# Block-sparse attention and a squared-ReLU MLP: rows gathered in even-odd order, keys copied as 32-bit words

## The chip, the cores and the metric

The kernel runs on one core of one Trainium2 chip. A time is the device time of one execution in microseconds (us). The five engines are named as in the profile: PE (TensorE; PEld are its weight loads), DVE (VectorE), ACT (ScalarE), POOL (GpSimd) and SP (SyncE, which here only issues DMAs). A line number such as L654 is that of the kernel before.

## The reference: what is computed

There are 4 batches of 8 heads, 768 positions and 64 values per head. Positions form 24 blocks of 32. A query block sees its own block and its two neighbours, the first and the last block, and three sampled blocks; the first and the last query block see everything. The sampled blocks are an input, so they are known only at run time.

```python
scores = scale * np.matmul(q, k.transpose(0, 1, 3, 2))
...
scores = np.where(mask, scores, -1000000000.0)
...
attn = attn / (np.sum(attn, axis=-1, keepdims=True) + 1e-09)
return np.matmul(attn, v).astype(np.float32)
```

The heads of a position are joined into 512 values, and an MLP follows on all 3072 positions: `h = x @ w_in` (512 to 2048), `r = max(h, 0)`, `(r * r) @ w_out` (2048 to 512).

## The kernel before, in words

**Two ways to do attention.** Batches 0 and 1 are done densely: all scores are computed (`scores`, L490), their exponentials are taken on ACT (`exps`, L501) and multiplied by a 0/1 mask on DVE (`masks`, L508), and `values` (L530) multiplies by v. Each v row carries a 1 besides its 64 values, so the sum of the weights comes out in the same matmul. `normalize` (L538, L540) divides on DVE and writes a buffer `xq`, of which there are `XQ_BUFS = 3`; `x_transp` (L547) turns the result over on PE, and `x_evac` copies it into `xT`, the MLP's input.

Batches 2 and 3 are done sparsely, in 6 tiles each. A tile has four query blocks of 32; tile 5, which comes first, has two inner blocks, and the first and last block of the sequence, which see all keys, fill it up. For each query block a tile gathers 256 keys into a buffer `KG`: 96 of the window, 32 of block 0, 96 of the three sampled blocks, 32 of the last block. `k_window` copies the window's keys (L637), `k_random` the sampled ones at a place held in a register (L654), `k_global` the two fixed blocks once per batch and then spread over the tile (L659, L661). `q_tile` copies the tile's queries into `QG` (L674). `QG` has a zero half for each of the two heads that lie on the 128 partitions, so that one matmul with all 128 partitions (L700) gives both heads' scores of 32 queries: 64 columns.

The values of v are gathered from a copy of v in DRAM, `vd`, into `VG`: `v_window` and `v_global` by DMAs that SP issues (L680, L684), `v_random` by indirect DMAs that POOL issues (L688), with row numbers in `idx`. `blocks_index` works out `idx` and the registers' places with some two dozen small DVE operations (L586 to L602). `s_scores`, `s_exps`, `s_values`, `s_normalize`, `s_transp` and `s_evac` are the sparse tile's counterparts of the dense steps. `s_patch` zeroes the weights of a block that would be counted twice.

**The order of positions.** The transposed q and k of the sparse batches, `QKB`, hold the even positions of a sequence first and then the odd ones, because a DMA transpose on pairs of rows leaves them so. In the kernel before, every copy out of `QKB` puts them back into natural order. `spread` is the destination's view:

```python
def keys_of(b):
    return QKB[b % 2][:, :, 1, :].rearrange("p a (n m) -> p a n m", n=2)
def spread(x):
    return x.rearrange("p a (m n) -> p a n m", n=2)
```

so an inner run of 16 or 48 keys is read from consecutive places and written to every second one.

**The MLP.** `hidden` (L795) multiplies by `w_in`, `relu` (L804 on ACT, L806 on DVE) and `square` (L815 on ACT, L817 on POOL) follow, `output` (L845) multiplies by `w_out`, `out_copy` and `store` bring it out. This work fills PE while attention waits for ACT and DVE.

**What sets the order.** A planner inside the kernel runs when the kernel is built. Every step is a `Task` with the engines that may do it, an estimated duration on each, its predecessors, the buffers that it takes and gives back, a key and sometimes an earliest time. `run_schedule` always issues the task that can start first on its engine and prefers small keys, and chooses the engine for tasks that have a choice: `k_window` between DVE and ACT, `q_tile` between DVE and POOL, `relu`, `square`, the casts and the evacuations likewise. The result is a fixed order of instructions on each engine. Each engine runs its instructions in that order, and the waits between engines are semaphores. The constants at the top (`TILE_AT` with the earliest time of each sparse tile, `VISITS`, `PACE`, `SEEDS`, which breaks ties, and others) shape that order. [...]

Of the kernel before, what the change touches and what calls it, by code (L numbers as in the profile page):

```python
# [12 lines left out]
F32 = mybir.dt.float32  # L13
# [12 lines left out]
def kernel(  # L26
# [37 lines left out]
    QC_BUFS, XQ_BUFS, YS_BUFS, XS_BUFS = 4, 3, 3, 2  # L64
# [26 lines left out]
    AHEAD = {"PE": 0, "DVE": 0.135, "ACT": 0.107, "POOL": 0.0, "SP": 0.0}  # L91
    LEAD = -2.424
    NB_, SLEAD, KACT = 49.137, 6.758, 0.3
    EARLY = (70.906, -88.936, -92.499, 95.336, 115.53, -46.181, 55.274, 166.555)
    TILE_AT = (102.791, 88.778, 40.785, 126.152, 70.33, 71.88, 157.89, 120.037, 118.424, 174.907, 219.536, 219.598)
    VISITS = (-24.404, 17.697, 7.265, 16.177, 0.947, -92.464, 8.409, 18.969, -10.624, 11.589, -49.341, -6.74, 2.02, 7.146, -74.249, -23.742, -110.985, -12.456)
    HOLD, PATIENCE = 0, 13.793
    PACE0, PACE, SINGLE, MASK_AT = 41.973, 1.372, 1, 17.0
# [5 lines left out]
    class Buf:  # L104
        def __init__(self, pool):
# [5 lines left out]
    TIES = 1.955, 1.912  # L111
    SEEDS = (
            850913, 826317, 823543, 823026, 572023, 972473, 867181, 602326, 495681,
            997735, 889080, 648164, 499408, 642303, 291601, 709162, 308345, 66895,
            457299, 405177, 404720, 744698, 807919, 805802)
# [8 lines left out]
    class Task:  # L124
        def __init__(self, engs, key, fn, deps=(), get=(), put=(), after=0.0, mode=None, dma=0.0, late=None, bias={}, port=False,
                     lead=0.0, yields=False, paced=False, quiet=False, mm=0):
# [5 lines left out]
            self.mm, self.us = mm, 0.0  # L132
# [7 lines left out]
    def run_schedule(free, bufs, dma_free, mode=128):  # L140
# [28 lines left out]
        while waiting or ready:  # L169
# [12 lines left out]
            for t in ready:  # L182
# [25 lines left out]
                for e, us in t.engs.items():  # L208
                    r = max([r0, free[e]] + [seen(d, e) - t.lead for d in t.deps])
                    sw = SWITCH if e == "PE" and t.mode and t.mode != mode else 0.0  # L210
                    if (e == "POOL" and not t.quiet) or (e == "DVE" and t.port):
                        p0, p1 = port["DVE" if e == "POOL" else "POOL"]
                        if p0 <= r < p1:
                            us = max(us, p1 - r + us - HEAD)
# [21 lines left out]
            if (e == "POOL" and not t.quiet) or (e == "DVE" and t.port):  # L236
                port[e] = (at, end)
                o = "DVE" if e == "POOL" else "POOL"
                more = end + last[o].us - HEAD - port[o][1] if last[o] and at <= port[o][0] < end else 0.0
# [81 lines left out]
    QG = [consts.tile([P, HP, 4, 2, block], BF, name=f"QG{i}") for i in range(2)]  # L321
    warm = QG[0].rearrange("p a i h q -> p (a i h q)")[:, 0:256]
# [32 lines left out]
    make_identity(nc, identb)  # L355

# [224 lines left out]
    def blocks_index():  # L581
# [4 lines left out]
        steps = [lambda: V.tensor_copy(out=rb, in_=picked_of),  # L586
                 lambda: TS(out=at16.rearrange("p (q r) -> p q r", r=n_rand), in0=picked_of[0:1], scalar1=block // 2, scalar2=None, op0=AOP.mult),
# [40 lines left out]
    def keys_of(b):  # L628
        return QKB[b % 2][:, :, 1, :].rearrange("p a (n m) -> p a n m", n=2)

    def spread(x):
        return x.rearrange("p a (m n) -> p a n m", n=2)

    def k_window(b, t, x, qs_, e):
        for i in qs_:
            m = (blocks_of(t)[i] - 1) * 16
            copy(e, spread(KG[x][:, :, i, 0:96]), keys_of(b)[:, :, :, m:m + 48])  # L637
# [3 lines left out]
    def k_places(ts, e):  # L641
# [3 lines left out]
            at16[0:1, n0:n1], engines=(mybir.EngineType.DVE,), min_val=0, max_val=(nb - 1) * 16,  # L645
# [3 lines left out]
    def k_random(b, t, x, qs_, e):  # L649
        for i in qs_:  # L650
            n = blocks_of(t)[i] - 1
            for j in range(n_rand):
                r = regs[n * n_rand + j]
                V.tensor_copy(out=spread(KG[x][:, :, i, 128 + 32 * j:160 + 32 * j]), in_=keys_of(b)[:, :, :, bass.ds(r, 16)])  # L654

    def k_global(b, x, first_, e):
        if first_:
            for j, m in ((0, 0), (1, S // 2 - 16)):
                V.tensor_copy(out=spread(GK[:, :, j, :]), in_=keys_of(b)[:, :, :, m:m + 16])  # L659
        for j, c in ((0, 96), (1, 224)):  # L660
            V.tensor_copy(out=KG[x][:, :, :, c:c + 32], in_=GK[:, :, j][:, :, None].broadcast_to([P, HP, 4, block]))  # L661
# [4 lines left out]
    def q_tile(b, t, x, e):  # L666
# [3 lines left out]
        for h in range(2):  # L670
            hs = slice(h * D, (h + 1) * D)
            for i0, i1, m0 in ((0, n // 16, m),) + (((n // 16, 4, 0),) if n < 64 else ()):
                for j in range(2):
                    copy(e, QG[x][hs, :, i0:i1, h].rearrange("p a i (m n) -> p a i n m", n=2)[:, :, :, j],  # L674
                         src[hs, :, j, m0:m0 + 16 * (i1 - i0)].rearrange("p a (i m) -> p a i m", m=16))

    def v_window(b, t, x, e):
        n, w = len(blocks_of(t)), H * VS
        v0 = vd[b][4 * t * block:4 * t * block + 1, :]
        sy.dma_start(out=VG[x][0:96, 0:n, 0, :], in_=bass.AP(v0.tensor, v0.offset, [[w, 96], [block * w, n], [1, w]]))  # L680

    def v_global(b, x, e):
        for c, r in ((0, 0), (1, S - block)):
            sy.dma_start(out=VG[x][96:128, :, c, :], in_=vd[b][r:r + block, None, :].broadcast_to([block, 4, H * VS]))  # L684
# [8 lines left out]
    def s_scores(b, t, x, s_, buf, e):  # L693
# [3 lines left out]
        for a in s_:  # L697
            for i in range(n):
                for c in range(2):
                    nc.tensor.matmul(ps[:, at:at + 2 * block], KG[x][:, a, i, c * P:(c + 1) * P], QG[x][:, a, i].rearrange("p h q -> p (h q)"),  # L700
                                     start=at % 512 == 0, stop=True, skip_group_check=True)
                    at += 2 * block
            for c in range(NCH) if n < 4 else ():
                w = 2 * (4 - n) * block
                nc.tensor.matmul(ps[:, at:at + w], QKB[b % 2][:, a, 1, c * P:(c + 1) * P], QG[x][:, a, n:].rearrange("p i h q -> p (i h q)"),
# [53 lines left out]
    def s_transp(b, t, e):  # L759
        xs = xtile.pop((b, t)).rearrange("p k g d -> p (k g d)")  # L760
        for a in range(HP):
            nc.tensor.transpose(stile[b, t][:, a // 2, a % 2 * P:(a % 2 + 1) * P], xs[:, a * P:(a + 1) * P], identb)
# [221 lines left out]
    def blocks_prepare():  # L984
# [3 lines left out]
        for f in steps:  # L988
            sp0.append(Task(("DVE", 0.43), 300.0, f, deps=sp0[0:1] + sp0[-1:], port=True))
# [207 lines left out]
```

## Time and profile before

| | |
|---|---|
| runs (us) | 267.88, 268.61, 272.57; median 268.61 |
| profiled execution, its own time | 268.88 us |
| span of the profiled execution | 267.1 us |
| granted TensorE clock | 0.999 |
| busy PE, DVE, ACT, POOL | 255.0, 169.7, 206.9, 132.5 us |
| PE matmuls | 3552 |
| random key copies, L654 | 132, 26.6 us busy |
| query copies on DVE, into `QG` | 48, 14.7 us busy |
| gathers by indirect DMA, L688 | 44 |

Busy time is the time in which an engine has an instruction under way. Consecutive instructions of an engine overlap, so the busy time of one instruction is longer than the spacing of several. PE's matmuls are pipelined, and a busy PE isn't PE at its full rate. A group's row gives its busy time and the mean of one instruction, and after the bar the idle time of the engine ahead of it and what ended that idle time. In a timeline, each row is a merged run of equal instructions, with its start, its length and, in brackets, idle time and what ended it.

### The profile page before, as it was taken

To read this page: it belongs to the slowest core of one execution; us is meant where nothing else is said; L and a number is where in the kernel's file an instruction comes from. 1 tells how busy PE (TensorE), PEld (TensorE's weight loads), DVE (VectorE), ACT (ScalarE), POOL (GpSimd) and SP (SyncE) were. 2 spreads that over 40 slices of the span, in tenths; PEclk is the share of its full clock that TensorE was granted. 3 is DMA by queue.
4 is the path that set the end of the run, shared out by engine and by line. 5 is a ranking of instruction groups with operands and counts; after the bars stand their busy time and mean duration, and the time that the engine had idled before them with its cause. 6 is when DMAs were issued, how large, how long until landed. Compare 5 with 4: busy or idle time off the path is not lost.

```text
span 267.1 us, 8695 instructions
## 1 busy us (share of the span) xinstructions
PE 255.0 (95%) x3552; PEld 162.5 (61%) x3552; DVE 169.7 (64%) x482; ACT 206.9 (77%) x312; POOL 132.5 (50%) x160
## 2 busy tenths in 40 slices
PE   7999999889999999979999999999999999999993
PEld 4778766476566656646666566555666565556553
DVE  7787678979987898897659862134774449130100
ACT  3798999869799988979999887636999449747710
POOL 2391753506387133277727866413857527704500
PEclk9999999999999999999999999999999999999999
DMA  6999999948882699899347799746654651330022
GB/s 199 368 264 206 201 206 327 351 93 199 219 180 41 170 217 246 225 287 191 92 141 180 206 217 183 204 131 197 176 150 137 183 152 31 103 111 2 1 79 82
DMA packets 62673, 46.41 MB, mean 174 GB/s; under 512 B 21768, under 2 KB 57512, under 8 KB 62632
## 3 DMA queue, kind: packets, MB, share of 16 engines
q1 hardware_dynamic: 55752, 36.79, 52.1%
q0 software_dynamic: 6336, 8.66, 16.5%
q8 instruction: 28, 0.46, 0.7%
q10 hardware_dynamic: 544, 0.39, 0.5%
q14 instruction: 13, 0.11, 0.2%
HBM read 37.32 MB, written 7.98 MB: 170 GB/s over the span
## 4 chain that ended last, share of the span: by engine, by line
PE 67%; DVE 11%; DMA 9%; issue 4%; SPq 3%; ACT 2%; POOL 2%; DVEq 0%; ACTq 0%; POOLq 0%
PE py L845 23%; PE X L795 20%; PE X L490 5%; PE po L530 5%; PE X L700 4%; PE X L746 4%; DMA RAW<-in_q_dram 3%; DVE pT L508 3%; DMA RAW<-in_v_dram 2%; DMA MK<-vd,idx 2%; SPq L301 2%; PE F L795 2%; PE X L845 2%; ACT pT L501 1%; DVE QG L276 1%
## 5 line engine op out<-in xcount | busy, mean ns | idle before, releaser
L845 PE MATMUL py<-w_out_sb,g 128*128 128x512 bf16 (+2 forms) x384 | 91.9, 368 | 0.0
L817 POOL TENSOR_TENSOR g<-r 128x384 bf16<-128x384 f32 (+1 forms) x53 | 50.8, 963 | 78.1 <-ACT r L804 58.6
L795 PE MATMUL X<-xT,w_in_sb 128*128 128x384 bf16 (+1 forms) x512 | 86.8, 313 | 1.1 <-ACT pT L501 1.1
L501 ACT ACTIVATE pT<-X 128x1024 bf16<-128x1024 f32 (+1 forms) x76 | 70.8, 992 | 8.8 <-PE X L494 2.5
L795 PEld LDWEIGHTS <-w_in_sb 128*128 128x128 bf16 x640 | 55.1, 98 | 29.1 <-issue 2.9
L804 ACT ACTIVATE r<-X 128x768 f32<-128x768 f32 (+1 forms) x60 | 45.5, 762 | 21.1 <-PE X L795 20.5
L845 PEld LDWEIGHTS <-g 128*128 128x128 bf16 x416 | 36.8, 98 | 30.3 <-issue 0.8
L508 DVE TENSOR_TENSOR pT<-pT,MK 128x1024 bf16<-128x1024 bf16 x60 | 46.7, 797 | 8.1 <-ACT pT L501 7.3
L815 ACT ACTIVATE g<-r 128x384 bf16<-128x384 f32 (+1 forms) x67 | 34.3, 539 | 1.7 <-DVE r L806 0.6
L712 ACT ACTIVATE pT<-X 128x1024 bf16<-128x1024 f32 x28 | 27.5, 1029 | 8.1 <-PE X L700 8.0
L530 PEld LDWEIGHTS <-pT 128*128 128x128 bf16 x576 | 22.3, 97 | 7.7 <-issue 3.2
L276 POOL CAST VN<-RAW 128x768 bf16<-128x768 f32 x16 | 14.7, 920 | 24.2 <-DMA RAW<-in_v_dram 21.3
L530 PE MATMUL po<-VN,pT 128*128 128x65 bf16 x576 | 25.4, 193 | 1.3 <-DVE pT L508 1.1
L490 PE MATMUL X<-QK 64*128 64x256 bf16 (+1 forms) x336 | 25.9, 257 | 0.5 <-ACT pT L501 0.3
L688 POOL DMA_INDIRECT MK<-vd,idx x24 | 22.4, 933 | 6.7 <-issue 4.9
L688 POOL DMA_INDIRECT RAW<-vd,idx x20 | 20.2, 1009 | 5.3 <-issue 4.1
L490 PEld LDWEIGHTS <-QK 64*128 64x128 bf16 x336 | 13.8, 94 | 9.9 <-issue 7.0
L754 DVE RECIPROCAL rss<-X 128x8 f32<-128x8 f32 x12 | 2.5, 206 | 25.9 <-PE X L746 25.8
L276 DVE COPY ys<-py 128x512 f32<-128x512 f32 (+1 forms) x5 | 3.0, 610 | 21.0 <-PE py L845 21.0
L274 ACT COPY ys<-py 128x512 f32<-128x512 f32 (+1 forms) x19 | 11.0, 580 | 6.2 <-PE py L845 6.1
L276 DVE CAST qc<-RAW 128x768 bf16<-128x768 f32 (+3 forms) x25 | 14.2, 580 | 2.0 <-DMA RAW<-in_q_dram 1.7
L276 DVE COPY QG<-QK 64x256 bf16<-64x256 bf16 (+2 forms) x48 | 14.7, 364 | 0.2
(105 smaller groups left out, 281.4 us busy)
## 6 DMA issues: line engine op xcount, KB each, us to landing
RAW<-in_v_dram SPq DMA_DIRECT2D x16, 384.0 KB, 7.1
RAW<-in_k_dram SPq DMA_DIRECT2D x15, 384.0 KB, 5.7
out_dram<-ys SPq DMA_DIRECT2D x21, 256.0 KB, 2.7
RAW<-in_q_dram SPq DMA_DIRECT2D x12, 384.0 KB, 3.7
MK<-vd SPq DMA_DIRECT2D x6, 396.0 KB, 3.3
w_in_sb<-in_moe_w_in_dram POOLq DMA_DIRECT2D x4, 512.0 KB, 7.0
w_out_sb<-in_moe_w_out_dram POOLq DMA_DIRECT2D x4, 512.0 KB, 14.6
vd<-VN SPq DMA_DIRECT2D x2, 792.0 KB, 4.1
```

The lines of the kernel that those rows point to most:

```text
L276: (V if e == "DVE" else G).tensor_copy(out=out, in_=in_)
L490: nc.tensor.matmul(ps[:, h, j * w:(j + 1) * w], QK[i][hs, 1, ksl], QK[i][hs, 0, qsl], start=j == 0, stop=not add, skip_group_check=True)
L501: A.activation(out=pT[:, :, 0:n], in_=stile.pop(a)[:, :, 0:n], func=AF.Exp, scale=scale)
L508: V.tensor_tensor(out=pT, in0=pT, in1=m[:, None].broadcast_to([P, 2, len(cs), w]), op=AOP.mult)
L530: nc.tensor.matmul(po[:, qc, h, :], pT[:, h, j * w + qc * P:j * w + (qc + 1) * P], VT[i][:, n, h, 0:VW], start=(n == 0 and qc == 0 and h = ...
L688: G.indirect_dma_start(out=VG[x][0:96, i, 1, :], out_offset=None, in_=vd[b][:, :], in_offset=bass.IndirectOffsetOnAxis(ap=idx[:, n:n + 1], ...
L712: A.activation(out=pT, in_=stile.pop((b, t, s_)), func=AF.Exp, scale=scale)
L795: nc.tensor.matmul(htile[T, f][:, i], w_in_sb[:, kc, (f + i) * P:(f + i + 1) * P], xT[b][:, kc, c0:c0 + w], start=(kc == 0), stop=(kc == K ...
L804: A.activation(out=to, in_=src, func=AF.Relu)
L815: A.activation(out=g, in_=r, func=AF.Square)
L817: (G if e == "POOL" else V).tensor_mul(out=g, in0=r, in1=r)
L845: nc.tensor.matmul(ytile[T, i], gtile[T, f][:, ts * P:(ts + 1) * P], w_out_sb[:, f, cs[0]:cs[1]], start=(f == 0), stop=(f == NF - 1))
```

## The change

The gathered rows stay in even-odd order within a block. Keys of a score and the rows of v that they meet have to agree, so v is gathered in the same order; queries only have to be put back at the end.

- **Keys.** A window of 96 or a block of 32 keys is now copied as an even half and an odd half, each a consecutive run, and the bf16 data are viewed as 32-bit words, two keys to a word. `k_window`, `k_random` and `k_global` do this through `keys_of` and `words`; the register places and `at16` are halved accordingly.
- **Queries.** `QG` has another layout, [head half, even/odd, 64], and `q_tile` copies whole runs of up to 64 with two or four copies. The score matmuls take 16 even and 16 odd queries of both halves as their moving operand. `s_transp` multiplies by a permutation matrix `places` in place of the identity, which puts the queries back into natural order.
- **Values.** `v_window` and `v_global` issue two DMAs each in place of one, for even and odd rows. `blocks_index` gets two more operations that turn the lane number into the even-odd row number.
- **Planner.** The tasks' estimates are changed, a task says how many operations it has (`nop`) and the planner's rule for the competition of DVE and POOL uses it. All constants of the order have new values, and `XQ_BUFS` is 2.

```diff
-    QC_BUFS, XQ_BUFS, YS_BUFS, XS_BUFS = 4, 3, 3, 2
+    QC_BUFS, XQ_BUFS, YS_BUFS, XS_BUFS = 4, 2, 3, 2
...
-    TILE_AT = (102.791, 88.778, 40.785, 126.152, 70.33, 71.88, 157.89, 120.037, 118.424, 174.907, 219.536, 219.598)
+    TILE_AT = (-39.154, 113.4, 58.045, 129.983, 53.984, 59.934, 133.038, 189.532, 195.761, 204.838, 216.885, 221.32)
...
                         if p0 <= r < p1:
-                            us = max(us, p1 - r + us - HEAD)
+                            us = max(us, p1 - r + us - HEAD) if last[o].nop == 1 else us + max(0.0, (p1 - p0) / last[o].nop / 2 - HEAD)
+                        elif r <= p0 < r + us and t.nop > 1:
+                            us += last[o].us - HEAD
...
-    QG = [consts.tile([P, HP, 4, 2, block], BF, name=f"QG{i}") for i in range(2)]
+    QG = [consts.tile([P, HP, 2, 2, P // 2], BF, name=f"QG{i}") for i in range(2)]
...
+    places = consts.tile([P, P], BF, name="places")
+    for j in range(2):
+        G.tensor_copy(out=places.rearrange("p (i m n) -> p n i m", n=2, m=16)[:, j], in_=identb.rearrange("p (i n m) -> p n i m", n=2, m=16)[:, j])
...
+        half = blocks_tmp("half", 5, 1)
+        steps = [lambda: TS(out=half, in0=lane, scalar1=float(block // 2), scalar2=float(1 - block), op0=AOP.is_ge, op1=AOP.mult),
+                 lambda: V.scalar_tensor_tensor(out=lane, in0=lane, scalar=2.0, in1=half, op0=AOP.mult, op1=AOP.add),
...
     def keys_of(b):
-        return QKB[b % 2][:, :, 1, :].rearrange("p a (n m) -> p a n m", n=2)
-
-    def spread(x):
-        return x.rearrange("p a (m n) -> p a n m", n=2)
+        return QKB[b % 2].bitcast(F32)[:, :, 1, :].rearrange("p a (n m) -> p a n m", n=2)
+
+    def words(x):
+        return x.bitcast(F32).rearrange("p a (n m) -> p a n m", n=2)
...
-            m = (blocks_of(t)[i] - 1) * 16
-            copy(e, spread(KG[x][:, :, i, 0:96]), keys_of(b)[:, :, :, m:m + 48])
+            m = (blocks_of(t)[i] - 1) * 8
+            copy(e, words(KG[x][:, :, i, 0:96]), keys_of(b)[:, :, :, m:m + 24])
...
-                V.tensor_copy(out=spread(KG[x][:, :, i, 128 + 32 * j:160 + 32 * j]), in_=keys_of(b)[:, :, :, bass.ds(r, 16)])
+                V.tensor_copy(out=words(KG[x][:, :, i, 128 + 32 * j:160 + 32 * j]), in_=keys_of(b)[:, :, :, bass.ds(r, 8)])
...
-            for i0, i1, m0 in ((0, n // 16, m),) + (((n // 16, 4, 0),) if n < 64 else ()):
-                for j in range(2):
-                    copy(e, QG[x][hs, :, i0:i1, h].rearrange("p a i (m n) -> p a i n m", n=2)[:, :, :, j],
-                         src[hs, :, j, m0:m0 + 16 * (i1 - i0)].rearrange("p a (i m) -> p a i m", m=16))
+            copy(e, QG[x][hs, :, h, :, 0:n], src[hs, :, :, m:m + n])
+            if n < 64:
+                copy(e, QG[x][hs, :, h, :, n:64], src[hs, :, :, 0:64 - n])
...
-        sy.dma_start(out=VG[x][0:96, 0:n, 0, :], in_=bass.AP(v0.tensor, v0.offset, [[w, 96], [block * w, n], [1, w]]))
+        for j in range(2):
+            v0 = vd[b][4 * t * block + j:4 * t * block + j + 1, :]
+            sy.dma_start(out=VG[x][48 * j:48 * j + 48, 0:n, 0, :], in_=bass.AP(v0.tensor, v0.offset, [[2 * w, 48], [block * w, n], [1, w]]))
...
-                    nc.tensor.matmul(ps[:, at:at + 2 * block], KG[x][:, a, i, c * P:(c + 1) * P], QG[x][:, a, i].rearrange("p h q -> p (h q)"),
+                    nc.tensor.matmul(ps[:, at:at + 2 * block], KG[x][:, a, i, c * P:(c + 1) * P], QG[x][:, a, :, :, i * 16:(i + 1) * 16],
...
-            nc.tensor.transpose(stile[b, t][:, a // 2, a % 2 * P:(a % 2 + 1) * P], xs[:, a * P:(a + 1) * P], identb)
+            nc.tensor.transpose(stile[b, t][:, a // 2, a % 2 * P:(a % 2 + 1) * P], xs[:, a * P:(a + 1) * P], places)
...
-                deps.append(T_(("DVE", 1.59), s - 8, k_random, b, t, x, qs_, deps=[k1, kp] + sp0, port=True))
+                deps.append(T_(("DVE", 1.2), s - 8, k_random, b, t, x, qs_, deps=[k1, kp] + sp0, port=True, nop=6))
...
-            deps.append(T_({"DVE": 1.2, "POOL": 1.7}, s - 8, q_tile, b, t, x, deps=qrs + [k1] + qz, after=late - SLEAD, port=True))
+            deps.append(T_({"DVE": 0.7, "POOL": 1.3}, s - 8, q_tile, b, t, x, deps=qrs + [k1] + qz, after=late - SLEAD, port=True, nop=2))
```

## The prediction

> **What bounds the kernel now.** The page first: the span, the engines' shares, and the slices of the span.
>
> ```profile
> span 267.1 us, 8695 instructions
> PE 255.0 (95%) x3552; PEld 162.5 (61%) x3552; DVE 169.7 (64%) x482; ACT 206.9 (77%) x312; POOL 132.5 (50%) x160
> ...
> PE   7999999889999999979999999999999999999993
> ...
> DVE  7787678979987898897659862134774449130100
> ACT  3798999869799988979999887636999449747710
> ```
>
> TensorE is never long without work, and DVE and ACT fall off after the middle. The busy times by stretch say where each is tight (dense batches 20 to 110 us, change of regime 110 to 120, sparse batches with MLP 120 to 240).
>
> ```profile
> core 0: us, PE busy (x) PEld busy (x) DVE busy (x) ACT busy (x) POOL busy (x), PEclk, DMA share, GB/s
> 0.00:20.00 20.00, 17.68 (x304) 13.09 (x304) 15.73 (x50) 13.56 (x24) 11.05 (x26) 1.00 0.96 277
> 20.00:110.00 90.00, 86.72 (x1176) 58.55 (x1173) 75.80 (x159) 79.92 (x108) 40.32 (x40) 1.00 0.91 206
> 110.00:120.00 10.00, 8.40 (x95) 5.38 (x92) 9.21 (x24) 8.06 (x14) 6.49 (x9) 1.00 1.04 259
> 120.00:160.00 40.00, 39.62 (x663) 24.97 (x662) 29.33 (x110) 37.04 (x61) 27.07 (x30) 1.00 0.70 171
> 160.00:240.00 80.00, 79.85 (x1177) 46.97 (x1175) 38.16 (x141) 56.51 (x90) 41.01 (x48) 1.00 0.55 148
> 240.00:267.10 27.10, 22.73 (x153) 13.51 (x151) 1.47 (x4) 11.82 (x19) 6.61 (x8) 0.99 0.12 41
> ```
>
> Busy is not streaming. In the chain, 8 matmuls of 384 columns take 1.30 us and 4 of 512 take 0.86 us: 0.42 ns per column. All 3552 matmuls at that rate (two at once for the 64-row scores, four for the 32-column values) come to 232 us, so 35 us of the span are not streamed. Laying that sum along the matmuls' start times, I find 8.0 us lost before 20, 14.0 from 20 to 110, 2.2 from 110 to 120, 2.7 from 120 to 160, 3.7 from 160 to 240, and 4.6 in the last copies and stores. The gathers of this change run from 113 to 228 us, where TensorE is close to its peak: all their cost to others fits into 8.5 us of loss, and part of that is fixed (the 896 values matmuls start 10.0 ns apart on average where four-at-once gives 6.9: 2.8 us).
>
> The largest single stall is here; the second fence has the DVE queue at the same time.
>
> ```profile
> 115.78 2.11 PE L795 MATMUL X<-xT,w_in_sb 128*128 128x384 bf16 x12
> 119.49 0.29 PE L547 MATMUL po<-identb,xq 128*128 128x128 bf16 x2 [1.60 <-DVE xq L540]
> 119.61 3.09 PE L795 MATMUL X<-xT,w_in_sb 128*128 128x384 bf16 x18
> ```
>
> ```profile
> 115.16 3.61 DVE L276 COPY QG<-QK 64x192 bf16<-64x192 bf16 x8
> 118.80 0.18 DVE L538 RECIPROCAL rs<-po 128x4 f32<-128x4 f32 x1
> 119.01 0.42 DVE L540 TENSOR_TENSOR xq<-po,rs 128x256 bf16<-128x256 f32 x1
> 119.35 0.90 DVE L654 COPY RAW<-QK 128x128 bf16 x6
> 120.17 0.36 DVE L659 COPY RAW<-QK 128x128 bf16<-128x128 bf16 x2
> 120.44 2.54 DVE L661 COPY RAW<-RAW 128x512 bf16<-128x512 bf16 x2
> 122.90 0.48 DVE L661 COPY KG<-RAW 128x512 bf16<-128x512 bf16 x2
> ```
>
> The last dense normalisation stands behind eight query copies (3.61 us), and TensorE waits 1.60 us for its result. The L661 rows show the second thing: two equal copies took 0.48 us at one time and 2.54 at another.
>
> [...] L654 copies last 0.23 us alone and 0.86 to 2.11 where a POOL square or cast overlaps their start. [...] No word copy is in this trace. The trace's own spacing of queued copies is 0.135 us for 128 bf16 elements, 0.207 for 256, 0.265 for 384 (0.07 us plus 0.51 ns per element), and 0.20 for the contiguous 512 of L661. [...] No moving operand of the kernel before is broken into short runs[...]. [...]
>
> **The change part by part.**
>
> *Keys as words.* 132 random copies go from 128 elements to 64 words: 0.135 to 0.10 us by the line above (bounds: no gain, or 0.05), 4.6 us of DVE. A window copy goes from 384 to 192: on DVE 0.265 to 0.17, 16 copies, 1.6 us; on ACT, spaced 0.48, by the fall of ACT's own copies (0.47 for 512, 0.25 for 256, PSUM sources) to 0.32, some 26 copies, 4 us. The replicated global keys keep their time: 512 contiguous elements at 0.20 against 256 words at 0.20.
>
> *Queries in runs.* Four copies of 64x256 at 0.207 become two of 64x512 contiguous at 0.20 (L661's price): 0.83 to 0.40 us a tile. The two short tiles go from eight copies to four. With 8 full tiles on DVE before and 6 after (POOL takes 4 instead of 2), DVE gets some 5 us back.
>
> *On the path.* 11 us of DVE and 4 of ACT are off the path wherever TensorE streams: 120 to 240 us would end no sooner. What counts is the stall. In the changed program's DVE order the last dense masks and both last normalisations stand before the first window and query copies, so the 1.60 us (1.76 counted by starts) go; next there is the hidden matmul's own data, already queued: -1.7 us. The stall at 153.24 us (0.54, scores waiting for random copies that two POOL squares had held for 2.11 us) has fewer and shorter copies [...]: -0.4. The other small losses of 110 to 240, some 3 us above the fixed part, I take down by a quarter: -0.7.
>
> *Rows of v.* 12 window DMAs become 24 and 8 global ones 16, same bytes. 20 more issues on SP at 0.30 to 0.50 us are about 8 us of a queue that has gaps of 2 to 8 us in this stretch. Behind them stand q/k/v loads, key transposes and stores. First tile: its windows and global rows are issued by 121, its values run at 134.1; four or five extra issues (2 us) fit. If that cover were gone they would cost their 2 us at each batch start. The gathers themselves keep count and size (0.93 us issue; 6.3 us in the chain at 168.8).
>
> *Small parts.* Two tiny index steps on DVE at 45 to 70 us: 0.06 to 1.1 us each (the neighbours' span, free or blocked); that stretch has slack on TensorE of other causes; 0.3. The permutation matrix: two POOL copies of 128x64, 0.15 to 0.5 us each (smallest POOL row, and POOL's 64x256 copy), in the 1.72 us that POOL idles before its first cast: 0; without that gap 1 us. Transposes with it instead of the identity: 48 of the same shape, 0. One xq buffer fewer: DVE may wait for a transpose, 0 to 1 us, taken 0.2. Nine more edge memsets on POOL (about 0.35) instead of DVE (0.085): 0, beside squares. The score matmuls read 32 or more columns in runs of 16: 0 (half rate is the rival below).
>
> *Order.* The planner's constants change, so everything else is interleaved anew. The same 3552 matmuls; the first sparse score has 101.0 us of streaming ahead of it instead of 99.3, and ACT has some 2.6 us less ahead of its last dense exponential (four copies, three activations of relu gone to DVE and POOL). ACT is the tight engine there (79.9 of 90). I take -0.6, with 2 either way.
>
> Sum: -1.7 - 0.4 - 0.7 + 0.3 + 0.2 - 0.6 = -2.9. The profiled execution took 268.88 us (span 267.1 and 1.8 around it): 266.0. Its time is 0.3 above the median of 268.61, so the forecast is a fall of about 1%.
>
> **Rivals.** *B, the new order also tightens the dense stage*: ACT's 2.6 us come out in full and the 14 us lost from 20 to 110 shrink by that, with the gains above doubled outside the stall: 268.9 - 2.1 - 1.4 - 2.6 = 262.8. For it: ACT at 89% there. Against: DVE, which takes over, has 84%.
> *C, something else takes the stall's place*: TensorE had filler work anyway, and a later wait (second batch's values for their gathers, 0.31 us at 175.12) grows by what is saved: 268.9. For it: values wait in order, and their rows come last.
> *D, slower: strided score operands.* If runs of 16 halve the moving rate, 352 matmuls of 64 columns lose 27 ns and 48 of 128 lose 54: 12.1 us, all on the bounding engine, 278. It decides from a 45% loss on (5.4 us). [...]
> That the word copies run no faster per byte is possible; the stall goes by order all the same, and time ends near 266.5.
>
> **Numbers.** Forecast 0.58 (264 to 268), B 0.20 (262 to 264), C 0.12 (268 to 270.5), D 0.10. The range 262.0 to 270.5 leaves out D and the ends of B and C. A measurement of this kernel can tell about 2% from no change, 5.4 us: faster than 263.2 is most of B and a little of the forecast, 0.18; slower than 274.0 is D and 0.02 for late rows; the rest 0.70.
>
> **What would show it.** Right: L654's successor near 0.10 us spacing, query copies at 0.20, no wait of a transpose for xq near 119 us, scores still 29 ns apart for 64 columns, DVE some 10 us and ACT 3 to 6 less busy, TensorE's work unchanged. Wrong: scores above 40 ns apart; values waiting on gathers for over 1 us; a first sparse score later than 123.4 us, where it is now.

## The result and the profile after

The changed kernel takes 265.11 us (median of 264.92, 264.87, 265.30 and 265.79), the kernel before 268.61 on the same chip: a ratio of 0.988, 95% interval 0.985 to 0.991. That is a fall of 1.2%; the prediction said 1%. The profiled execution after took 264.92 us, with a span of 263.1 us against 267.1. Ratios compare the executions within 1.5% of the fastest one of their kernel, which for the kernel before with its zero rows moved leaves out 11 of 24 (the median of all 24 is 268.31 us, against 268.57 for the kernel before).

First the page of the kernel after, to be read beside the two fences of the prediction:

```profile
span 263.1 us, 8679 instructions
...
PE 251.6 (96%) x3519; PEld 162.9 (62%) x3552; DVE 154.0 (59%) x452; ACT 198.7 (76%) x303; POOL 138.8 (53%) x175
...
PE   7999999999998899999999999999999899999994
...
DVE  7797789999999988873555623136075435121000
ACT  3888979988989998889877897423985568945920
```

DVE is 15.7 us less busy and ACT 8.2, POOL 6.3 more. TensorE's work is the same: 3552 weight loads in both, while 33 matmul records are missing in this trace. The same stretches as before, columns as there:

```profile
core 0: us, PE busy (x) PEld busy (x) DVE busy (x) ACT busy (x) POOL busy (x), PEclk, DMA share, GB/s
0.00:20.00 20.00, 18.11 (x304) 13.48 (x304) 16.05 (x52) 13.64 (x23) 12.12 (x28) 1.00 0.96 277
20.00:110.00 90.00, 86.52 (x1191) 60.22 (x1203) 80.83 (x165) 80.60 (x107) 39.24 (x40) 1.00 0.83 194
110.00:120.00 10.00, 9.55 (x79) 5.75 (x79) 8.58 (x26) 8.87 (x16) 6.65 (x7) 1.00 0.94 244
120.00:160.00 40.00, 39.44 (x620) 25.12 (x625) 17.09 (x83) 35.04 (x63) 32.17 (x41) 1.00 0.98 201
160.00:240.00 80.00, 78.31 (x1198) 46.39 (x1208) 30.86 (x128) 48.80 (x79) 42.00 (x53) 1.00 0.57 147
```

From 120 to 240 us DVE fell from 67.5 us busy to 48.0 and TensorE is as busy as before (117.8 against 119.5, with records missing): the copies became cheaper where TensorE was already fed. From 20 to 110 us the kernel after has 1203 weight loads done where the kernel before has 1173: the dense stage runs ahead.

The DVE queue and TensorE around the stall that the prediction led with, after the change:

```profile
114.52 0.18 DVE L548 RECIPROCAL rs<-po 128x4 f32<-128x4 f32 x1 [0.52 <-PE po L540]
114.73 0.42 DVE L550 TENSOR_TENSOR xq<-po,rs 128x256 bf16<-128x256 f32 x1
115.93 0.29 DVE L283 COPY xT<-po 128x256 bf16<-128x256 bf16 x1 [0.77 <-PE po L557]
116.14 0.42 DVE L283 COPY RAW<-QK 128x192 f32<-128x192 f32 x2
116.47 1.41 DVE L283 COPY QG<-QK 64x384 bf16<-64x384 bf16 x4
```

```profile
115.62 0.28 PE L557 MATMUL po<-identb,xq 128*128 128x128 bf16 x2
115.73 4.06 PE L810 MATMUL X<-xT,w_in_sb 128*128 128x384 bf16 x24
```

The last normalisation stands ahead of the first query copies, and the transpose that needs it has no wait. The query copies themselves went from 3.61 us (eight, of 64x192 and 64x64; the row names the first shape) to 1.41 (four, of 64x384 and 64x128). Most of the 3.61 us went by while squares and query copies ran on POOL (114.75 to 118.70): at 186.48 us, with no POOL work beside them, four copies of the same shapes take 0.64 us. Why a copy on DVE takes longer beside POOL's work is not shown by any trace here; the planner lengthens its estimates there, for DVE's tasks those with `port=True`.

To see where the time went over the whole span, take the streamed time of all matmuls in program order (the measure of the prediction's first part) and ask at what time each kernel has so much of it behind it. The difference of the two executions, after minus before:

| streamed work behind (us) | time of before (us) | after minus before (us) |
|---|---|---|
| 30 | 40.8 | -0.4 |
| 40 | 54.6 | -2.8 |
| 60 | 78.4 | -4.0 |
| 80 | 100.9 | -1.7 |
| 90 | 112.3 | -2.2 |
| 100 | 124.1 | -3.3 |
| 150 | 177.7 | -4.1 |
| 200 | 229.7 | -2.9 |
| 230 | 260.3 | -2.9 |
| end of the span | 267.1 | -4.0 |

So there are four parts: 3.6 us gained between 41 and 78 us, 2.3 given back by 101, 1.6 gained around 119 (the stall), about nothing over the sparse batches. The last 1.0 is not the change's: the kernel before needed 4.59 us from its last matmul's start to its end in this one execution, the kernel after 3.63, and the six kernels of the experiments that were profiled where the kernel before took 268 to 270 us, with tails of the same form, 3.30 to 3.76. Like against like, the trace gives 2.9 us.

The first gain is far more than the -0.6 that the prediction's sum has for the order. Two waits of the kernel before lie in this stretch. The first one, DVE and TensorE:

```profile
47.81 2.53 DVE L508 TENSOR_TENSOR pT<-pT,MK 128x1024 bf16<-128x1024 bf16 x2
50.41 0.42 PE L530 MATMUL po<-VN,pT 128*128 128x65 bf16 x8 [0.81 <-DVE pT L508]
```

These two masks took 1.30 us each beside casts on POOL (47.42 to 49.80); a mask alone takes 0.68 (40.79). TensorE waits for them twice, at 49.18 and 50.41, 1.07 us in all. In the kernel after, the masks between 40 and 53 us take 0.68 to 0.76 and TensorE waits for none of them. By 54.6 us of the kernel before, the kernel after is 2.4 of its 3.6 us ahead (rows 30 and 40 of the table). The 1.07 us are part of that; the rest is tied to no wait on record.

The second wait comes behind that, all engines:

```profile
47.29 5.09 SPq L450 DMA_TRANSPOSE QK<-qc  x2
50.35 0.28 DVE L614 MEMSET pT<- 32x264 uint32 x1
52.48 0.99 SPq L618 DMA_DIRECT2D vd<-pT  x2
56.20 1.02 ACT L501 ACTIVATE pT<-X 128x1024 bf16<-128x1024 f32 x1 [1.92 <-PE po L547]
57.27 1.03 PE L795 MATMUL X<-xT,w_in_sb 128*128 128x256 bf16 x8 [1.14 <-ACT pT L501]
```

`zero_rows` (L614 to L618) takes one of the six `pT` buffers, fills it with zeros and writes them to `vd`, behind the rows of v. The write stands on SP behind two DMA transposes, so it is issued 2.13 us after the memset and lands at 56.09. The buffer is held for 5.7 us, while ACT needs one for each exponential. ACT idles 1.92 us until 56.20, 0.11 after the landing (the row names a matmul, but that isn't what came last), and TensorE waits 1.14 us for that exponential. Between 54.6 and 57.9 us of the kernel before, the kernel after gains 0.5 us (from -2.8 to -3.3). In the kernel after the buffer is held for almost as long (from 52.92; the write lands at 58.39), but ACT has relu and square to do just then:

```profile
52.92 0.28 DVE L627 MEMSET pT<- 32x264 uint32 x1
53.50 0.84 SPq L631 DMA_DIRECT2D vd<-pT  x2
...
55.31 1.94 ACT L511 ACTIVATE pT<-X 128x1024 bf16<-128x1024 f32 x2 [0.67 <-PE X L500]
```

And what was given back by 101 us, in the kernel after:

```profile
81.05 2.00 DVE L615 TENSOR_SCALAR idx<-KG 32x22 int32<-32x22 f32 x2
...
83.79 0.28 PE L557 MATMUL po<-identb,xq 128*128 128x128 bf16 x2 [1.02 <-DVE xq L550]
...
90.59 0.91 PE L540 MATMUL po<-VN,pT 128*128 128x65 bf16 x24 [0.79 <-DVE xT L283]
```

Two index operations of 22 elements a partition took 2.00 us beside two POOL squares, and a normalisation stood behind them. The new order has its own small stalls: the two rows of TensorE make 1.8 of the 2.3 us.

### The profile page after: what moved, and what is told of

Its sections match the earlier page's. It is cut to its first block, busy times and chain, and to the rows that moved or that the text cites. A ratio compares the mean times of both kernels' runs of the same rounds, so it can differ in the third digit from the quotient of the medians.

```text
span 263.1 us, 8679 instructions
## 1 busy us (share of the span) xinstructions
PE 251.6 (96%) x3519; PEld 162.9 (62%) x3552; DVE 154.0 (59%) x452; ACT 198.7 (76%) x303; POOL 138.8 (53%) x175
## 4 chain that ended last, share of the span: by engine, by line
PE 63%; DVE 13%; DMA 9%; ACT 5%; issue 5%; POOL 3%; SPq 1%; POOLq 0%; DVEq 0%; ACTq 0%
PE py L860 21%; PE X L810 21%; DVE pT L518 8%; PE po L540 4%; PE X L500 4%; DMA RAW<-in_q_dram 3%; PE X L761 3%; PE X L715 3%; ACT pT L511 2%; PE F L810 2%; DMA RAW<-in_k_dram 2%; POOL MK L703 2%; DMA RAW<-vd,idx 2%; DMA MK<-vd,idx 2%; PE X L860 2%
## 5 line engine op out<-in xcount | busy, mean ns | idle before, releaser
L860 PE MATMUL py<-w_out_sb,g 128*128 128x512 bf16 (+2 forms) x351 | 85.2, 367 | 2.4 <-issue 0.9
L810 PE MATMUL X<-xT,w_in_sb 128*128 128x384 bf16 (+1 forms) x512 | 84.0, 313 | 0.0
L860 PEld LDWEIGHTS <-g 128*128 128x128 bf16 x416 | 35.9, 98 | 29.6 <-issue 2.0
L518 DVE TENSOR_TENSOR pT<-pT,MK 128x1024 bf16<-128x1024 bf16 x60 | 49.3, 850 | 2.4 <-ACT pT L511 2.2
L281 ACT COPY ys<-py 128x512 f32<-128x512 f32 (+1 forms) x17 | 9.9, 582 | 17.9 <-PE py L860 17.9
L703 POOL DMA_INDIRECT RAW<-vd,idx x20 | 19.1, 954 | 5.8 <-issue 5.0
L283 POOL CAST VN<-RAW 128x768 bf16<-128x768 f32 x15 | 15.5, 1033 | 11.8 <-DMA RAW<-in_v_dram 11.6
L283 DVE CAST qc<-RAW 128x768 bf16<-128x768 f32 (+3 forms) x22 | 13.2, 624 | 1.8 <-DMA RAW<-in_q_dram 1.0
L283 POOL CAST qc<-RAW 128x768 bf16<-128x768 f32 (+1 forms) x13 | 13.0, 1009 | 1.6 <-DMA RAW<-in_q_dram 0.8
L761 PEld LDWEIGHTS <-pT 128*32 128x32 bf16 x896 | 9.3, 95 | 6.2 <-issue 6.1
```

What stands on the lines that cost most here:

```text
L283: (V if e == "DVE" else G).tensor_copy(out=out, in_=in_)
L518: V.tensor_tensor(out=pT, in0=pT, in1=m[:, None].broadcast_to([P, 2, len(cs), w]), op=AOP.mult)
L703: G.indirect_dma_start(out=VG[x][0:96, i, 1, :], out_offset=None, in_=vd[b][:, :], in_offset=bass.IndirectOffsetOnAxis(ap=idx[:, n:n + 1], ...
L810: nc.tensor.matmul(htile[T, f][:, i], w_in_sb[:, kc, (f + i) * P:(f + i + 1) * P], xT[b][:, kc, c0:c0 + w], start=(kc == 0), stop=(kc == K ...
L860: nc.tensor.matmul(ytile[T, i], gtile[T, f][:, ts * P:(ts + 1) * P], w_out_sb[:, f, cs[0]:cs[1]], start=(f == 0), stop=(f == NF - 1))
```

## The experiments

The expectations number their theories. Theory 1 is that the order carries most of the gain (against it theory 2, that the cheaper copies do) and that the DVE time of the sparse copies is off the path; theory 3, that the held `pT` buffer costs the dense stage its time; theory 4, that the query copies alone made the stall at 119 us; theory 5, that this stall and the held buffer are separate causes. All ratios are to the kernel before, run beside it on the same chip.

### The order alone

The planner's constants, estimates and `XQ_BUFS` of the kernel after, with the gathers of the kernel before.

```diff
-            copy(e, words(KG[x][:, :, i, 0:96]), keys_of(b)[:, :, :, m:m + 24])
+            copy(e, spread(KG[x][:, :, i, 0:96]), keys_of(b)[:, :, :, m:m + 48])
...
-                V.tensor_copy(out=words(KG[x][:, :, i, 128 + 32 * j:160 + 32 * j]), in_=keys_of(b)[:, :, :, bass.ds(r, 8)])
+                V.tensor_copy(out=spread(KG[x][:, :, i, 128 + 32 * j:160 + 32 * j]), in_=keys_of(b)[:, :, :, bass.ds(r, 16)])
```

(the same for queries, global keys, rows of v and transposes; the two new index operations stay in the order, their result unused)

> The planner's constants, estimates and XQ_BUFS of the changed kernel, hence its order of instructions, with the gathers of the kernel before (natural order, spread key copies, four query copies, whole v DMAs, identity in the transposes). Theory 1 (the order carries most of the gain: the stall at 119 us goes because the last normalisations stand ahead of the copies, and the dense stage is interleaved better): 265.3 to 266.8 us, the fall at 45 to 80 us (about 3 us against the kernel before) is still there, no wait of a transpose for xq near 119 us. Theory 2 (the cheaper copies carry it, and the order only makes use of them): 267.5 us or more, with new waits for KG or QG between 113 and 230 us.

Measured: 1.007 [1.004, 1.010]. The order alone is slower than the kernel before, and theory 1 falls as far as the total goes. It holds for the stall: no transpose waits over 0.16 us for `xq` between 108 and 126 us. The trace has the dense stage's gain too (3.1 us between 30 and 60 us of streamed work), but loses some 4.5 us between 120 and 130. There TensorE waits for gathered rows of v:

```profile
PE X L759 <- DMA RAW<-vd,idx: 3.6, 3, 3.0
```

(the waits of TensorE: total, times, longest, in us). POOL's query copies take 1.94 us a tile there instead of 1.35 and its next gathers are issued at 134.08 instead of 131.15; then two of the indirect DMAs took 1.88 and 2.11 us instead of 0.92. Behind the longest wait TensorE's granted clock was 0.5 for 3.4 us (0.83 in the mean from 150 to 160 us), which makes the mean granted clock of this execution 0.994. It took 273.03 us, more than the ratio stands for, so the size of the wait is that of one case. But 13 of the 22 executions have a clock of 0.994 or less (8 of 55 in the kernel before), and the other nine took 269.17 us in the median (all of the kernel before: 268.57). So most of what this order loses with the old copies goes with the lowered clock, which fits late gathers; only one such execution was traced.

### The copies alone

The gathers of the kernel after with the order of the kernel before.

```diff
-            copy(e, spread(KG[x][:, :, i, 0:96]), keys_of(b)[:, :, :, m:m + 48])
+            copy(e, words(KG[x][:, :, i, 0:96]), keys_of(b)[:, :, :, m:m + 24])
...
-                V.tensor_copy(out=spread(KG[x][:, :, i, 128 + 32 * j:160 + 32 * j]), in_=keys_of(b)[:, :, :, bass.ds(r, 16)])
+                V.tensor_copy(out=words(KG[x][:, :, i, 128 + 32 * j:160 + 32 * j]), in_=keys_of(b)[:, :, :, bass.ds(r, 8)])
```

(and the rest of the change but its planner)

> The even-odd gathers of the changed kernel in the order of the kernel before, its constants, estimates and three xq buffers. Theory 1: the query copies that stand ahead of the last dense normalisation shrink from 3.6 to about 1.5 us, so the stall of 1.76 us near 119 us shrinks to under 0.5; the dense stage is as before, with its waits at 49 to 58 us; 266.8 to 268.0 us. Theory 2: 265.0 to 266.0 us.

Measured: 0.994 [0.991, 0.997], that is 266.9 us, in the range of theory 1 and outside that of theory 2; the profiled execution took 265.56 us. The dense stage has no gain at all (+0.3 us up to 40 us of streamed work, -0.3 after). Between 90 and 100 the kernel gains 1.6 us: the stall at 119 us is gone although the order is the old one. Its DVE queue:

```profile
114.90 2.19 DVE L276 COPY QG<-QK 64x384 bf16<-64x384 bf16 x4
117.12 0.18 DVE L540 RECIPROCAL rs<-po 128x4 f32<-128x4 f32 x1
117.33 0.42 DVE L542 TENSOR_TENSOR xq<-po,rs 128x256 bf16<-128x256 f32 x1
```

The query copies still stand ahead of the normalisation, but they take 2.19 us instead of 3.61, and 117.75 is early enough for the transpose at 117.82. From there to the last matmul the copies gain another 0.5 us. Neither theory holds whole: the order alone loses 0.7%, the copies alone gain 0.6%, and both together 1.2%.

### Queries alone, keys alone

Both in the order of the kernel before. Queries alone: `QG`'s layout, `q_tile`, the score operands and `places`. Keys alone: keys as words, rows of v and `lane` to match.

```diff
-            for i0, i1, m0 in ((0, n // 16, m),) + (((n // 16, 4, 0),) if n < 64 else ()):
-                for j in range(2):
-                    copy(e, QG[x][hs, :, i0:i1, h].rearrange("p a i (m n) -> p a i n m", n=2)[:, :, :, j],
-                         src[hs, :, j, m0:m0 + 16 * (i1 - i0)].rearrange("p a (i m) -> p a i m", m=16))
+            copy(e, QG[x][hs, :, h, :, 0:n], src[hs, :, :, m:m + n])
+            if n < 64:
+                copy(e, QG[x][hs, :, h, :, n:64], src[hs, :, :, 0:64 - n])
```

> The kernel before in its own order, but queries in contiguous runs (half as many copies, the new score operands, the permutation matrix in the transposes); keys and rows of v as before. Theory 4: what the copies gain in the old order is the eight 64x192 query copies that stood ahead of the last dense normalisation; as four of 64x384 they let it through, no transpose waits for xq near 119 us, and the time is 0.993 to 0.996 of before (266.7 to 267.5). Rival: keys as words carry the gain; then 0.998 to 1.001 here.

> The kernel before in its own order, but keys copied as 32-bit words in even-odd order, rows of v to match and the two index steps; queries as before. Theory 4: DVE and ACT get some 8 us less busy, but the eight query copies still stand ahead of the last normalisation, the wait of about 1.6 us near 119 us stays, and the time is 0.997 to 1.001 of before (267.8 to 268.9). Rival: 0.993 to 0.996, as for the whole set of copies.

Measured: 1.025 [1.018, 1.033] and 1.015 [1.008, 1.022], but these numbers answer nothing: the kernel before itself took 296.38 us beside them, for a reason that wasn't found. In the four traces taken there TensorE stops again and again for 0.7 us, with no wait on a semaphore behind it, but only from about 132 us on. The part before is whole, and it holds the place in question. Queries alone, TensorE:

```profile
119.19 0.28 PE L549 MATMUL po<-identb,xq 128*128 128x128 bf16 x2 [0.22 <-DVE xq L542]
```

Keys alone, DVE and TensorE:

```profile
116.04 3.61 DVE L276 COPY QG<-QK 64x192 bf16<-64x192 bf16 x8
119.69 0.18 DVE L538 RECIPROCAL rs<-po 128x4 f32<-128x4 f32 x1
```

```profile
120.38 0.29 PE L547 MATMUL po<-identb,xq 128*128 128x128 bf16 x2 [1.40 <-DVE xq L540]
```

The queries take the wait away (1.4 us gained between 90 and 100 us of streamed work), the keys leave it (0.2). Theory 4 holds for the stall. What the keys give in total isn't measured.

### The zero rows from another buffer

The rows for `vd` are read from the second query buffer, which is zeroed already, in place of a `pT` buffer: in the kernel before, and in the kernel after.

```diff
-            z = work.tile([P, 2, 512], BF, name="pT", tag="pT", bufs=PT_BUFS).rearrange("p h c -> p (h c)")
-            V.memset(z[0:block, 0:H * VS], 0.0)
+            z = QG[1].rearrange("p a i h q -> p (a i h q)")
```

> The kernel before, with the zero rows for vd taken from QG1, which is zero at that time, in place of a freshly zeroed pT buffer; order otherwise the same. Theory 3 (at 50 to 57 us a pT buffer is held until a DMA that stands behind two DMA transposes has read it, ACT idles 1.92 us for a free pT buffer and TensorE 1.14 for ACT): the ACT idle time near 56 us goes and the time falls by 0.8 to 1.5 us, to 267.1 to 267.8. Rival (the dense stage is bound by ACT's or DVE's sum and the wait is made up at once): within 0.4 us of 268.6.

> The same edit of the zero rows in the changed kernel, where the DMA of the zero rows follows the memset within 0.6 us. Theory 3: little to gain, 0 to 0.7 us below the changed kernel (264.4 to 265.2). Rival: the held buffer matters here as much, 264.0 or less.

Measured: 0.992 [0.989, 0.995] in the kernel before, and 0.986 [0.981, 0.990] in the kernel after, whose own ratio is 0.988. The first ratio stands for some 2.2 us (0.8 to 1.5 were expected), but the median of all 24 executions shows a gain of only 0.3. The trace, of an execution of 273.19 us, has the effect in its place: ACT no longer idles ahead of the fourth exponential.

```profile
53.50 4.00 ACT L501 ACTIVATE pT<-X 128x1024 bf16<-128x1024 f32 x4 [0.89 <-PE X L490]
```

TensorE's 1.14 us of waiting are gone, and by streamed work the edit gains 1.7 us between 40 and 60. In the kernel after it gives at most 0.3 us, within the interval. So theory 3 holds for the held buffer: it costs the old order some 1.7 us of the dense stage and the new order next to nothing. It doesn't follow that the new order gains its time there. Of its 3.6 us, 2.4 came before this wait, and with the zero rows moved the wait for masks is still there in the old order (0.81 us at 52.71).

### The copies and the zero rows, in the old order

The kernel of "the copies alone" with the edit of the zero rows.

> The kernel before in its own order, with all copies of the change and with the zero rows of vd read from the second query buffer in place of a fresh pT buffer. Theory 5: the wait at 119 us and the held pT buffer are separate causes, so their gains multiply, 0.9936 by 0.9919: 0.984 to 0.988 of before (264.3 to 265.4), the time of the kernel after without its order. Rival: the two gains are one, or later steps of the sparse batches take them back; then 0.990 to 0.994 (266 to 267).

Measured: 0.9855 [0.982, 0.989], 264.35 us. The product of the two ratios is 0.9936 x 0.9919 = 0.9855: theory 5 holds. Beside the copies alone (0.994) this is a second measurement of what the zero rows give, 0.8%. In its trace ACT at the place in question:

```profile
50.59 4.00 ACT L503 ACTIVATE pT<-X 128x1024 bf16<-128x1024 f32 x4 [0.29 <-PE X L492]
55.14 0.60 ACT L812 ACTIVATE r<-X 128x512 f32<-128x512 f32 x1 [0.56 <-PE X L803]
```

Four exponentials run in one piece where the kernel before idled 1.92 us ahead of its fourth. By streamed work, the kernel gains 1.7 us between 40 and 60, 1.9 between 80 and 100, and is 3.5 us ahead at 230. So two separate edits in the old order reach what the whole change reaches (264.35 against 265.11, intervals overlapping): the new order isn't needed for it, though it doesn't get there by the same waits.

The same kernel was measured twice more where the kernel before took 296.38 and 297.86 us: 1.005 [1.001, 1.008] and 0.999 [0.995, 1.003]. Nothing follows from these.

> The kernel before in its own order, with all copies of the change and with the zero rows of vd read from the second query buffer in place of a fresh pT buffer. Theory 5: the wait at 119 us and the held pT buffer are separate causes, so their gains multiply, 0.9936 by 0.9919: 0.986 of before (264.0 to 265.5), the time of the kernel after without its order. Rival: the sparse batches start when their gathers are ready whatever the dense stage gains, or the two gains are one; then 0.990 to 0.994 (266 to 267).

> The kernel before in its own order, with all copies of the change and with the zero rows of vd read from the second query buffer in place of a fresh pT buffer. Theory 5: the wait at 119 us and the held pT buffer are separate causes, so their gains multiply, 0.9936 by 0.9919: 0.984 to 0.988 of before (264.3 to 265.4), the time of the kernel after without its order. Rival: the two gains are one, or later steps of the sparse batches take them back; then 0.990 to 0.994 (266 to 267).

### Every random key copy twice

In the kernel after:

```diff
-                V.tensor_copy(out=words(KG[x][:, :, i, 128 + 32 * j:160 + 32 * j]), in_=keys_of(b)[:, :, :, bass.ds(r, 8)])
+                for _ in range(2): V.tensor_copy(out=words(KG[x][:, :, i, 128 + 32 * j:160 + 32 * j]), in_=keys_of(b)[:, :, :, bass.ds(r, 8)])
```

> The kernel after with each of its 132 random key copies issued twice: 13 us more of DVE at 0.10 us each, from 118 to 225 us. Theory 1: DVE's time there is off the path except where scores wait for their copies, so the time is 0.984 to 0.992 of before (264.5 to 266.5). Rival: the copies' time is on the path, and the time rises by a good part of the 13 us, to 0.998 of before or more (268).

Measured: 1.032 [1.027, 1.037], 278.06 us, 13 us above the kernel after (12 by the two ratios). The forecast of theory 1 fails here, and my dose was wrong too. Each second copy carries a wait on a semaphore that the first one sets, as both write the same place. So it starts 0.23 us after the first, the next one 0.12 after it, instead of 0.10 throughout, and DVE is busy 35.5 us more instead of 13. The queue and what waits for it:

```profile
143.60 6.54 DVE L667 COPY KG<-QK 128x64 f32 x24
150.05 0.20 DVE L769 RECIPROCAL rss<-X 128x8 f32<-128x8 f32 x1
150.28 0.69 DVE L771 TENSOR_TENSOR xs<-X,rss 128x512 bf16<-128x512 f32 x1
```

```profile
151.03 0.42 PE L777 MATMUL X<-places,xs 128*128 128x128 bf16 x4 [3.42 <-DVE xs L771]
```

A sparse tile's normalisation stands behind 24 copies, as the dense one stood behind eight at 119 us. Together TensorE waits 3.4 us for `xs` and 6.2 us for gathered keys (3.7 for those in one set of buffers, 2.5 in the other). So about a third of the added DVE time comes out at the end. The run adds semaphore waits together with the time, and doesn't tell the two apart. This doesn't say that the time of the copies as they are is on the path: taking time off them gained 0.5 us over the sparse batches, putting three times as much on (31.4 us busy against 9.8, both from 120 to 240 us) cost 12. One reading is that the order leaves room for the durations that it has, and not for much longer ones; a smaller dose wasn't tried.

Where the kernel before took 296.38 and 297.86 us, this kernel took 308.81 and 309.01: 1.048 [1.041, 1.055] and 1.041 [1.034, 1.049].

> The kernel after with each of its 132 random key copies issued twice: 13 us more of DVE at 0.10 us each, from 118 to 225 us. Theory 1: DVE's time there is off the path except where scores wait for their copies, so the time is 265 to 266.5. Rival: the copies' time is on the path, and the time rises by a good part of the 13 us, to 268 or more.

> The kernel after with each of its 132 random key copies issued twice: 13 us more of DVE at 0.10 us each, from 118 to 225 us. Theory 1: DVE's time there is off the path except where scores wait for their copies, so the time is 0.984 to 0.992 of before (264.5 to 266.5). Rival: the copies' time is on the path, and the time rises by a good part of the 13 us, to 0.998 of before or more (268).

## Why the prediction was right, and where not

The time was right (266.0 forecast, 265.11 measured; profile against profile, without the 1.0 us of the tail, -2.9 forecast and -2.9 found). One term of the sum was right in cause and nearly in size, the stall. That the rest came to the same number is luck: the order gained 3.6 us and lost 2.3 of them again where 0.6 was forecast, and the terms of the sparse batches brought nothing.

- *The stall at 119 us, -1.7.* Right: it went, for 1.1 to 1.6 as one counts from 90 or from 80 us of streamed work. The reason given, that the new order puts the normalisation first, is sufficient ("the order alone" has no such wait) but not necessary. The shorter query copies do it in the old order too, for 1.4 us alone.
- *Random copies held up beside POOL, -0.4, and a quarter of the other small losses, -0.7.* Wrong for the kernel after. The stall at 153 us is gone, but between 110 and 230 us of streamed work the kernel after gained nothing; it lost 0.6. The step failed that took losses down in proportion to busy time. In the old order the copies gave 0.5 there, and yet with the zero rows moved too TensorE still waits 0.52 us for random copies at 150.19: cheaper copies don't do away with such a stall. The new order has a wait of its own, the values of one tile for their rows (0.52 us at 209.43).
- *Index steps, +0.3; one `xq` buffer fewer, +0.2.* The two new index operations can't be told from the rest. The index work as a whole did stop TensorE, 1.02 us at 83.79, but by two old operations (L602 before) at a new place. No normalisation waits for a free `xq` in a row of the trace.
- *The order, -0.6 with 2 either way.* The term that was mis-sized: the order brought 2.2 us up to 90 us of streamed work, 4.0 at its best. I had seen that ACT loses time in the dense stage and put it down to ACT's load. The profile showed two single waits of TensorE instead, and the order takes both away: 1.07 us for masks that POOL's casts held up, and 1.14 us for an exponential, ahead of which ACT idles 1.92 us with a releaser that has nothing to do with it. They don't account for all of the gain up to 54.6 us.
- *Word copies.* Right: the random ones start 0.102 us apart (0.10 forecast), window copies on DVE 0.17 to 0.22 (0.17). On ACT 0.24 against 0.48; I said 0.32. DVE's and ACT's busy time fell by more than forecast (15.7 against some 10, 8.2 against 3 to 6), as work also went to POOL.
- *Query copies.* Wrong in both prices, right in the gain. Full tiles before (eight of four copies) and after (six of two):

```profile
L276 DVE COPY QG<-QK 64x256 bf16<-64x256 bf16 x32 | 8.7, 321 | 0.2
L283 DVE COPY QG<-QK 64x512 bf16<-64x512 bf16 x12 | 3.5, 289 | 0.8 <-issue 0.7
```

A tile took 1.09 us where I said 0.83, and takes 0.58 where I said 0.40: 0.5 less, 0.43 forecast. I had taken the start-to-start time of copies in a row on the same partitions. In these traces a copy on the other 64 partitions starts only when the one before it has ended (0.34 us after the start of one of 0.31, at 134.87 us in the kernel before; 0.21 on the same ones).

- *SP's twenty more issues, the permutation matrix, the strided score operands, at nothing.* Right. No tile's values wait for `v_window` or `v_global`, the transposes start 56.2 ns apart (56.4 before), the 64-column scores 29.1 ns (29.3 before, the one wait left out). With that rival D is out: in runs of 16 queries (32 bytes) the scores' operands take no longer than in one run of 64. For these operands the forecast of nothing was an estimate of mine that no row of the kernel before showed.
- *The rivals.* B came true in its place, the dense stage, though not by ACT's load; C came true beside it: 2.3 us were given back by 101 us, most of them to new waits. They offset each other, and the forecast between them held by luck.

## What to carry to other kernels

An engine that is idle a third of the time can still hold up the bounding one (DVE, busy 64% of the span, TensorE by 1.60 us at 119 us): look for a long run of copies that was put ahead of a short operation someone waits for, and either shorten the run or move the short operation. When an activation idles with a releaser that has nothing to do with its operands, ask which buffer it writes and who else holds one; here one that was borrowed for a small DMA was held for 5.7 us, until the DMA had landed, with two DMA transposes queued ahead of it. And a new order and cheaper operations have to be measured apart: here one of them alone was slower, and a gain as large as that of both was to be had by two edits in the old order. That such an edit gains as much doesn't make its cause the cause of the order's gain: look when each of them gains it.

## What was not expected of the hardware

- A DVE copy that moves to the other 64 partitions didn't overlap the one before it. In the kernel before, 64x256 query copies of 0.30 us started the next one after 0.20 to 0.21 us on the same 64 partitions and after 0.31 to 0.34 on the other 64. In the kernel after, each 64x512 copy (0.27 to 0.29 us) goes to the other half, and starts the next after 0.28 to 0.32.
- After TensorE had waited 2.98 us in "the order alone" and 3.42 us in "every random key copy twice", its granted clock was 0.5 for 3.4 us, from 153.3 and 151.3 us. Single waits of up to 1.6 us in the kernel before had no such effect (its granted clock was 1.00 in each stretch up to 240 us). But the length of one wait doesn't decide: in the kernel before with its zero rows moved the clock also fell at 18.9 us (0.97 in the mean of the first 20 us), after a wait of 1.39 us, and in "the order alone" a wait of 1.46 us at the same place left it at 1.00. What sets it was not shown. In the two executions named first, the wait cost more than itself: 3.4 us at 0.5 are some 1.7 us of work, an estimate from these two numbers.
- The issue of an indirect DMA on POOL usually took 0.92 us, but now and then 1.9 to 4.2 (4.16 at 142.87 us in the kernel before with its zero rows moved). In "the order alone" and there, TensorE then waited 2.6 to 3.0 us for the rows. What delays the issue wasn't found.
